# Attention of a fused kernel: both heads of a pair side by side on the array

## The chip, the cores and the metric

The kernel runs on one core of a Trainium2 chip. The metric is the device time of one execution in microseconds, measured on that core, as the median of several runs.

## What is computed

Three stages follow each other. The inputs q, k and v have 2 batches, 8 heads, 576 places and 64 dimensions a head, in float32.

```python
def _attn_ref(q, k, v):
    ...
    q_rot, k_rot = (rotate(q), rotate(k))
    scale = 1.0 / np.sqrt(D)
    scores = scale * np.matmul(q_rot, k_rot.transpose(0, 1, 3, 2))
    scores = scores - np.max(scores, axis=-1, keepdims=True)
    attn = np.exp(scores)
    attn = attn / (np.sum(attn, axis=-1, keepdims=True) + 1e-09)
    return np.matmul(attn, v).astype(np.float32)
...
def _moe_ref(x, w_in, w_out):
    h = x @ w_in
    g = np.maximum(0.01 * h, h)
    return (g @ w_out).astype(np.float32)
```

`rotate` turns the two halves of a head's dimensions by cosine and sine of the place. The attention output, 1152 rows of 512, goes through the dense stage above (512 to 2048 to 512), and then through eight experts (512 to 1024 to 512), of which each row takes the two with the largest noisy logits. The change touches attention alone.

## The kernel before

Attention works on eight pairs of heads (`NP = B * 4`). A pair's q and k are loaded (`load_qk`), turned by place on VectorE or GpSimd (`rope`, letters O and P), transposed on TensorE (`turn`, Q and K), and split into a high part on ScalarE (`turn_high`, h and i) and a rest on VectorE (`turn_low`, j and n), both in float32r, a float32 that TensorE reads in one pass. TensorE contracts over 128 rows, a head has 64 dimensions. So `TQ` and `TK` hold a head's parts twice, in the upper and the lower 64 rows: high and low of q against two copies of high k, then low k against a second copy of high q, with the row of negated maxima below it. The second copies are made by DMA (`turn_copy`, a and b).

The work on a tile of 128 keys or queries, in steps:

- `max_scores` (M), line 386: scores with queries as rows, two matmuls of 288 columns; `max_reduce` (D), line 393, takes the negated maximum on VectorE.
- `max_turn` (R), lines 403 to 408, makes the column of maxima a row; `max_rows` (m) and `max_put` (e) bring it into `TQ`.
- `scores` (S), line 437: keys as rows, two products for each half of 288 queries. `exp` (W), line 443, on ScalarE.
- `values` (V), line 456: float32, 128 keys against 128 columns, of which 64 are values and 64 are ones, so that the sums come out beside the values. A float32 matmul stands in the trace as two passes.
- `take` (U), `sums` (t), `invert` (T), `sums_out` (s), `sums_in` (B), `normalize` (N), `x_high` and `x_low` (X, Y): divide by the sums and write the dense stage's input. Of the last pair, T, s, B and N are queued in the dense stage, at its second step, X and Y at the third.

Maxima, scores and turned tiles take turns in three buffers of PSUM (the digit behind a letter). The order of all engines' work in attention is written out by hand in the string `ORDER`, a letter for each step, and each engine runs its own instructions in that order. The order brings the maxima of the next pair in between the scores and values of this one. Weights of the dense stage are loaded and converted under it (F, and the signs at the end). Pair 0 starts apart: VectorE turns its head 0 and GpSimd its head 1; TensorE runs `busy` matmuls on zeros meanwhile (line 140).

Of the kernel before, what the change touches and what calls it, by code (L numbers as in the profile page):

```python
# [45 lines left out]
def constants():  # L46
# [11 lines left out]
    for j in range(KT):  # L58
        ok = p if j < 4 else p[:64]
        s = 4 * ok + j if j < 4 else 512 + ok  # L60
        ct[ok, j] = np.concatenate([cos[s], cos[s]], 1)
        st[ok, j] = np.concatenate([-sin[s], sin[s]], 1)
# [20 lines left out]
def fused_kernel(ctx, tc, q, k, v, w_in, w_out, w_gate, w_noise, noise, w1, w2, consts, out):  # L83
# [59 lines left out]
    NSLOT = 12  # L143
    slots = [[epool.tile([128, 2, 512], F32R, name=f"w{n}_0") for n in "hl"]]
    KQ, KK = 2 * 2 * KT * 128, 2 * 2 * S
    last_set = [epool.tile([128, n], F32R, name=f"set_{x}") for x, n in (("q", KQ), ("k", KK))]
    for t in last_set:
        slots.append([t[:, o:o + 1024].rearrange("p (a b) -> p a b", a=2) for o in (0, 1024)])
# [83 lines left out]
    NSET = 3  # L232
# [4 lines left out]
    raw, TQ, TK, VF, VT = [], [], [], [], []  # L237
    for i in range(NSET):
        if i < 2:
            TQ.append(ap.tile([128, 2, 2, KT * 128], F32R, name=f"TQ{i}"))  # L240
            TK.append(ap.tile([128, 2, 2, S], F32R, name=f"TK{i}"))
        else:
            TQ.append(last_set[0].rearrange("p (a w n) -> p a w n", a=2, w=2))
            TK.append(last_set[1].rearrange("p (a w n) -> p a w n", a=2, w=2))
    maxes = []
    for i in range(2):
        raw.append({n: ap.tile([128, 2, KT, D], F32, name=f"raw_{n}{i}") for n in "qk"})
        VF.append(ap.tile([128, 4, 192], F32, name=f"VF{i}"))
        VT.append(ap.tile([128, 2, 128], F32, name=f"VT{i}"))
        maxes.append(ap.tile([128, 9], F32R, name=f"maxes{i}"))  # L250

    def fill(eng, t, v):
        if eng == "A":
            src = (one if v else zero)[:t.shape[0]]
            for _ in t.shape[2:]:
                src = src[:, :, None]
            A.copy(t, src.to_broadcast(t.shape))
        else:
            (V if eng == "D" else G).memset(f32(t), v)

    def fill_raw(i, n):
        G.memset(raw[i][n][64:128, :, 4, :], 0.0)

    def fill_t(i, n):
        t, v = ((TQ[i][0:64, 1, 1, :], 0.0), (TK[i][0:64, 1, 1, :], 0.0), (TK[i][64:65, 0, 1, :], 1.0),
                (TK[i][0:1, 1, 1, :], 1.0))[n]
        fill(FILL_T[i], t, v)

    def fill_v(i, n):

        t, v = ((VF[i][:, :, 64:128], 1.0), (VT[i][0:64, 0, 64:128], 1.0), (VT[i][64:128, 0, :], 0.0),
                (VT[i][64:128, 1, 0:64], 1.0), (VT[i][0:64, 1, :], 0.0))[n]
        fill(FILL_V[i], t, v)

    def load_qk(pr, n, part, a=slice(0, 2), queue=None):

        b, h0 = divmod(pr, 4)
        h0 *= 2
        src, t = q if n == "q" else k, raw[pr % 2][n]
        base = src.offset + (b * H + h0 + a.start) * S * D  # L280
        heads = [S * D, a.stop - a.start]
        if part == 0:
            (queue or nc.sync).dma_start(t[:, a, 0:4, :].rearrange("p h j d -> p h (j d)"),
                                         bass.AP(tensor=src.tensor, offset=base, ap=[[4 * D, 128], heads, [1, 4 * D]]))
        else:
            (queue or nc.sync).dma_start(t[0:64, a, 4, :],
                                         bass.AP(tensor=src.tensor, offset=base + 512 * D, ap=[[D, 64], heads, [1, D]]))

    def load_v(pr, part):
# [3 lines left out]
        if part < 2:  # L293
            nc.sync.dma_start(VF[pr % 2][:, :, part * 128:part * 128 + 64],
                              bass.AP(tensor=v.tensor, offset=base + part * S * D, ap=[[4 * D, 128], [D, 4], [1, D]]))
        else:
            a = part - 2
            nc.sync.dma_start(VT[pr % 2][a * 64:a * 64 + 64, a, a * 64:a * 64 + 64],
# [21 lines left out]
    pause = ap.tile([1, 1], F32, name="pause")  # L320

    def after_first():

        G.tensor_copy(pause, roped[0, "k"][0][0:1, 0, 0, 0:1])

# [4 lines left out]

    def turn(pr, n, a, at):


        r = roped[pr, n][0]
        p = ps(at, "pT", (128, 1024))
# [5 lines left out]
        for b in range(2) if a is None else (a,):  # L341
            turned[pr, n, b] = p

    def sides(a):
        return slice(64 * a, 64 * a + 64), slice(64 - 64 * a, 128 - 64 * a)

    def turn_high(pr, n, a):
        here = sides(a)[0]
        A.activation((TQ if n == "q" else TK)[pr % NSET][here, a, 0, 0:S], turned[pr, n, a][here, 0:S], AF.Copy)

    def turn_copy(pr, n, a):
        here, there = sides(a)
        t = (TQ if n == "q" else TK)[pr % NSET]
        if (pr, n) == (0, "k"):
            A.activation(t[there, a, 0, 0:S], turned[pr, n, a][here, 0:S], AF.Copy)
        elif n == "k":
            nc.sync.dma_start(f32(t)[there, a, 0, :], f32(t)[here, a, 0, :])
        else:
            nc.sync.dma_start(f32(t)[here, a, 1, 0:S], f32(t)[here, a, 0, 0:S])

    def turn_low(pr, n, a):
        here, there = sides(a)
        t = (TQ if n == "q" else TK)[pr % NSET]
        o = t[there, a, 0, 0:S] if n == "q" else t[here, a, 1, :]
        V.tensor_tensor(o, turned[pr, n, a][here, 0:S], f32(t)[here, a, 0, 0:S], op=OP.subtract)  # L365

    def tiles(pr):
        last = ((0, 4), (1, 4)) if pr == 0 else ((None, 4),)  # L370
        return [(0, j) for j in range(4)] + list(last) + [(1, j) for j in range(4)]

    def part(a, j):

        if j < 4:
            return ((a, j * 128, 128),), slice(0, 128)
        return (((1, 448, 128), (0, 512, 64)) if a is None else ((0, 512, 64),) if a == 0 else ((1, 448, 128),),
                slice(0, 128) if a is None else slice(64 * a, 64 * a + 64))

    maxed = {}  # L380
# [8 lines left out]
    def max_reduce(pr, a, j):  # L389
        rows = part(a, j)[1]  # L390
        i = 4 if j == 4 else j if a == 0 else 5 + j
        with nc.allow_low_precision(reason="what is taken off is the same in a row's every place"):
            V.tensor_reduce(maxes[pr % 2][rows, i:i + 1], maxed.pop((pr, a, j))[rows, :, 0:288], axis=AX.XY, op=OP.max,  # L393
                            negate=True)
# [3 lines left out]
    def max_turn(pr, a, at):  # L398
        m = maxes[pr % 2]
        if (pr, a) in DIRECT:  # L400
            p = rows[pr, a] = ps(at, "pR", (128, 1024))
            for j in range(4):
                T.matmul(p[:1, j * 128:(j + 1) * 128], m[:, 5 * a + j:5 * a + j + 1], ident_r, start=True, stop=True)
            r = slice(64 * a, 64 * a + 64)
            T.matmul(p[:1, 512:576], m[r, 4:5], ident_r[r, r], start=True, stop=True)
        else:
            p = rows[pr, a] = ps(at, "pR", (128, 128), F32R)
            T.transpose(p[:5, :], m[:, 4 * a:4 * a + 5], ident_r)

    def max_rows(pr, a):  # L410
        o = 64 - 64 * a
        if (pr, a) in DIRECT:
            A.activation(TQ[pr % NSET][o:o + 1, a, 1, 0:S], rows[pr, a][:1, 0:S], AF.Copy)
        else:
            mr = a2.tile([16, 128], F32R, name="mr")
            A.activation(mr[:5], f32(rows[pr, a])[:5], AF.Copy)
            rows[pr, a] = mr

    def max_put(pr, a, w):
        t, mr = f32(TQ[pr % NSET]), f32(rows[pr, a])  # L420
        if a == 0:
            nc.sync.dma_start(t[64:65, 0, 1, :].rearrange("o (j n) -> o j n", j=KT), mr[0:5, :])
        elif w == 0:
            nc.sync.dma_start(t[0:1, 1, 1, 0:512].rearrange("o (j n) -> o j n", j=4), mr[1:5, :])
        else:
            nc.sync.dma_start(t[0:1, 1, 1, 512:576], mr[0:1, 64:128])
# [754 lines left out]
```

## Time and profile before

| | |
|---|---|
| median of 3 runs | 663.74 us (663.44 to 664.36) |
| span of the profiled execution | 663.5 us |
| TensorE busy | 641.5 us, 97% |
| VectorE, ScalarE, GpSimd busy | 394.5, 318.7, 166.3 us |
| attention, first maxima to last values | 9.9 to 175.6 us |

The profiled execution is one run; its span is from the first to the last instruction, and the runs' median lies 0.2 us above it. A busy engine in this table is one that has an instruction in flight. TensorE's matmuls overlap in the listing, so busy time is not the same as streaming time: the distance from one start to the next says what a matmul costs.

### The profile page before, as it was taken

What the parts mean: (1) busy time and instruction counts of PE and PEld (TensorE: products, weight loads), DVE (VectorE), ACT (ScalarE), POOL (GpSimd) and SP (SyncE); (2) the same over time, 40 slices, a digit from 0 to 9 for tenths busy, and PEclk for the clock granted to TensorE, in tenths of its full rate; (3) what the DMA queues carried; (4) which work ended last, traced back from release to release, by engine and by line L of the source; (5) the groups of instructions that cost most, each with busy time, mean ns of one, the idle gap of its engine ahead of it and who ended that gap; (6) DMA issues with size and microseconds to landing.
All of it is one profiled execution on the core that took longest, in us unless ns stands there. A gap on an engine that the chain in (4) does not pass through costs nothing. (4 is left out here: it accounts for less than half of the span.)

```text
span 663.5 us, 10447 instructions
## 1 busy us (share of the span) xinstructions
PE 641.5 (97%) x3676; PEld 552.9 (83%) x3680; DVE 394.5 (59%) x835; ACT 318.7 (48%) x646; POOL 166.3 (25%) x176
## 2 busy tenths in 40 slices
PE   7999999999999999999999999999999999999993
PEld 4778888888878888889799966888888888888893
DVE  8754554687269888853146663565565656475611
ACT  5455554676545554432235432545454545454511
POOL 7985555121130000000000003041505050505102
PEclk9899999999999999999999999999999999999998
DMA  6434422666358443310355432566658584757423
GB/s 172 119 89 120 101 65 67 178 187 196 114 180 301 142 127 126 112 33 1 116 191 154 119 103 61 160 158 185 174 169 201 157 211 146 193 158 197 101 31 42
DMA packets 88903, 90.56 MB, mean 136 GB/s; under 512 B 21455, under 2 KB 66702, under 8 KB 88846
## 3 DMA queue, kind: packets, MB, share of 16 engines
q1 hardware_dynamic: 83502, 78.67, 40.3%
q0 software_dynamic: 4608, 10.49, 8.0%
q10 hardware_dynamic: 736, 0.69, 0.3%
q8 instruction: 30, 0.49, 0.3%
q14 instruction: 27, 0.22, 0.1%
HBM read 69.95 MB, written 14.19 MB: 127 GB/s over the span
## 5 line engine op out<-in xcount | busy, mean ns | idle before, releaser
L218 DVE TENSOR_TENSOR wl<-raw,wh 128x512 fp32r<-128x512 f32 x108 | 72.6, 688 | 53.3 <-ACT wh L216 49.4
L1036 POOL DMA_INDIRECT out<-y_row,idx x24 | 41.9, 1744 | 174.4 <-ACT y_row L1023 169.5
L216 ACT ACTIVATE wh<-raw 128x512 fp32r<-128x512 f32 x108 | 66.4, 629 | 37.1 <-DMA raw<-in_moe_w 36.5
L393 DVE TENSOR_REDUCE maxes<-pM 128x1 fp32r<-128x576 f32 (+1 forms) x73 | 53.9, 754 | 44.5 <-PE pM L386 43.8
L903 POOL DMA_INDIRECT got<-x_rows,idx x24 | 25.1, 1046 | 215.8 <-DVE load L853 199.7
L1012 PE MATMUL bank<-wh,g_x 128*128 128x512 f32 x216 | 78.0, 403 | 0.2
L456 PE MATMUL pO<-p,VF 128*128 128x288 f32 x256 | 72.4, 409 | 0.8 <-ACT p L443 0.8
L443 ACT ACTIVATE p<-pS 128x576 f32<-128x576 f32 (+1 forms) x73 | 46.6, 650 | 51.7 <-PE pS L437 51.0
L599 PE MATMUL bank<-xe_h,wl 128*128 128x320 f32 x216 | 67.0, 311 | 0.0
L599 PE MATMUL bank<-xe_h,wh 128*128 128x320 f32 x216 | 66.8, 310 | 0.0
L599 PE MATMUL bank<-xe_l,wh 128*128 128x320 f32 x216 | 66.3, 309 | 0.0
L620 ACT ACTIVATE g_t<-bank 128x512 f32<-128x512 f32 (+2 forms) x48 | 23.5, 490 | 86.3 <-PE bank L599 86.3
L621 DVE TENSOR_TENSOR g_f<-bank,g_t 128x512 f32<-128x512 f32 (+2 forms) x48 | 26.7, 557 | 50.1 <-ACT g_t L620 49.8
L456 PEld LDWEIGHTS pO<-p,VF 128*128 128x128 f32 x256 | 45.4, 190 | 9.7 <-ACT p L443 1.3
L599 PE MATMUL bank<-xh,wh 128*128 128x384 f32 (+2 forms) x152 | 51.6, 340 | 1.4 <-ACT xh L506 1.4
L608 PE MATMUL bank<-g_h,wh 128*128 128x384 f32 (+2 forms) x152 | 51.9, 341 | 0.0
L599 PE MATMUL bank<-xl,wh 128*128 128x384 f32 (+2 forms) x152 | 51.3, 338 | 0.2 <-POOL xl L512 0.2
L599 PE MATMUL bank<-xh,wl 128*128 128x384 f32 (+2 forms) x152 | 51.4, 338 | 0.0
L608 PE MATMUL bank<-g_l,wh 128*128 128x384 f32 (+2 forms) x152 | 51.3, 337 | 0.0
L608 PE MATMUL bank<-g_h,wl 128*128 128x384 f32 (+2 forms) x152 | 51.0, 336 | 0.0
L1012 PEld LDWEIGHTS bank<-wh,g_x 128*128 128x128 f32 x216 | 40.5, 188 | 7.9 <-DVE g_x L995 0.5
L437 PE MATMUL pS<-TQ,TK 128*128 128x288 f32 (+1 forms) x240 | 45.2, 319 | 1.8 <-DVE TQ L365 0.9
(240 smaller groups left out, 1470.1 us busy)
## 6 DMA issues: line engine op xcount, KB each, us to landing
raw<-in_moe_w SPq DMA_DIRECT2D x128, 256.0 KB
raw<-in_moe_w_in SPq DMA_DIRECT2D x16, 512.0 KB
raw<-in_moe_w_out SPq DMA_DIRECT2D x16, 512.0 KB
inv_sum<-inv_sums SPq DMA_DIRECT2D x16, 144.0 KB
out<-none SPq DMA_DIRECT2D x9, 256.0 KB
VF<-in_v SPq DMA_DIRECT2D x16, 128.0 KB
wl<-kept SPq DMA_DIRECT2D x4, 512.0 KB
wh<-kept SPq DMA_DIRECT2D x4, 512.0 KB
```

Of the source, the lines that this page charges most:

```text
L216: A.activation(hi[:, part], t, AF.Copy)
L218: V.tensor_tensor(lo[:, part], t, f32(hi)[:, part], op=OP.subtract)
L393: V.tensor_reduce(maxes[pr % 2][rows, i:i + 1], maxed.pop((pr, a, j))[rows, :, 0:288], axis=AX.XY, op=OP.max, negate=True)
L437: T.matmul(p[:m, z, 0:288], tk[:r, b, w, c:c + m], tq[:r, b, w, z * 288:(z + 1) * 288], start=(w == 0), stop=(w == 1), skip_group_check=True)
L443: A.activation(t[r], scored.pop((pr, a, j))[r, :, 0:288], AF.Exp, scale=0.125)
L456: T.matmul(acc[g][:, z, 0:288], w, p[r, z, :], start=opens, stop=closes)
L599: T.matmul(h[:, :n], w[:, 0, k * 128:(k + 1) * 128], m[:, k, cols:cols + n], start=(i == 0), stop=(i == 11))
L608: T.matmul(b[:, o:o + n], w[:, 1, ds], m[:, :n], start=(first and opens and t == 0), stop=(last and t == 2), skip_group_check=True)
L621: V.tensor_tensor(g[:, :n], h[:, :n], t[:, :n], op=OP.max)
L903: G.indirect_dma_start(out=t[:n], out_offset=None, in_=x1_rows, in_offset=bass.IndirectOffsetOnAxis(ap=idx[e][:n, st:st + 1], axis=0))
L1012: T.matmul(yr[st], s, w, start=(f == 0 and t == 0), stop=(f == 7 and t == 2))
L1036: s = G.indirect_dma_start(out=out, out_offset=bass.IndirectOffsetOnAxis(ap=idx[e][:n, st:st + 1], axis=0), in_=r[:n], in_offset=None, com ...
```

## The change

Two heads of a pair lie beside each other, head 0 in rows 0 to 63 and head 1 in rows 64 to 127 of one `high` and one `low` tile for each of q and k. No part is stored twice.

- Maxima and scores are matmuls on 64 rows. Each comes twice in a row, once for each head, on the two halves of the rows and into two banks of PSUM. Maxima now come from the high parts alone, and of pairs 1 to 7 in column pieces of 320 and 256. Scores are four products: high with high, low q, low k, and a matrix of ones with the row of maxima `MR`.
- Values are four float32 matmuls of 32 columns each, two for each head, in four places of the array's columns. Ones no longer stand beside the values: sums are matmuls of their own against `add_up`, 144 columns wide, again four side by side.
- One `take`, one copy of sums and no `turn_copy` or `max_put` are left of those steps. Constant tiles are filled on GpSimd. GpSimd turns all pairs from pair 1 on, VectorE also head 1's q of pair 0. The last pair's T, s and B are queued one dense step sooner. `ORDER` is new.

```diff
-    def max_scores(pr, a, j, at):
-        p = maxed[pr, a, j] = ps(at, "pM")
-        for b, c, m in part(a, j)[0]:
-            for z in range(2):
-                T.matmul(p[:m, z, 0:288], TQ[pr % NSET][:, b, 0, c:c + m],
-                         TK[pr % NSET][:, b, 0, z * 288:(z + 1) * 288], start=True, stop=True, skip_group_check=True)
+    def here(a):
+        return slice(0, 128) if a is None else slice(64 * a, 64 * a + 64)
...
+    def max_scores(pr, i, j, at):
+        p = maxed[pr, i, j] = ps(at, "pM")
+        hq, hk = high["q"][pr % NSET], high["k"][pr % NSET].rearrange("p (j w n) -> p j w n", j=KT, w=2)
+        for a, z in ((i, 0), (i, 1)) if pr == 0 else ((0, i), (1, i)):
+            o = (192, 0)[z] if pr == 0 else 0
+            n = (320, 256)[z]
+            T.matmul(p[:, z if pr == 0 else a, o:o + n], hq[here(a), j * 128:(j + 1) * 128],
+                     hk[here(a), 0:KT - z, (a + z) % 2], start=True, stop=True)
...
+    def max_turn(pr, at):
+        p = rows[pr] = ps(at, "pR", (128, 1024))
+        for j in range(KT):
+            T.matmul(p[:65, j * 128:(j + 1) * 128], peak[pr % 2][:, j], ident_r, start=True, stop=True)
...
-    def scores(pr, a, j, at):
-        tq, tk = TQ[pr % NSET], TK[pr % NSET]
-        p = scored[pr, a, j] = ps(at, "pS")
-        for b, c, m in part(a, j)[0]:
-            for w in range(2):
-                r = 65 if w == 1 and b == 0 else 128
-                for z in range(2):
-                    T.matmul(p[:m, z, 0:288], tk[:r, b, w, c:c + m], tq[:r, b, w, z * 288:(z + 1) * 288],
-                             start=(w == 0), stop=(w == 1), skip_group_check=True)
+    def products(pr, j):
+        i = pr % NSET
+        cs = slice(j * 128, j * 128 + 128)
+        return ((high["k"][i][:, cs], high["q"][i]), (high["k"][i][:, cs], low["q"][i]),
+                (low["k"][i][:, cs], high["q"][i]), (ones[:, int(j == 4)], MR[pr % 2]))
+    def scores(pr, j, z, at):
+        p = scored[pr, j, z] = ps(at, "pS")
+        cols = slice(z * 288, z * 288 + 288)
+        ws = products(pr, j)
+        for t, (w, x) in enumerate(ws):
+            for a in range(2):
+                T.matmul(p[:, a, 0:288], w[here(a)], x[here(a), cols], start=(t == 0), stop=(t == 3))
...
-        w = VF[pr % 2][:, j, 64 * a:64 * a + 128] if j < 4 else VT[pr % 2][r, a, :]
-        for z in range(2):
-            T.matmul(acc[g][:, z, 0:288], w, p[r, z, :], start=opens, stop=closes)
+        for a in range(2):
+            for c in range(2):
+                w = VF[pr % 2][:, a, j] if j < 4 else VT[pr % 2][:, a]
+                r = slice(64 * a + 32 * c, 64 * a + 32 * c + 32)
+                T.matmul(y[r, z, 0:288], w[:, 32 * c:32 * c + 32], prob[pr, j, z][:, a], start=(j == 0), stop=False, skip_group_check=True)
+        for o in range(2 * z):
+            for a in range(2):
+                for c in range(2):
+                    r = slice(64 * a + 32 * c, 64 * a + 32 * c + 32)
+                    T.matmul(y[r, o, 288:432], add_up[:, 0 if j < 4 else 1 + a], prob[pr, j, c][:, a, o * 144:o * 144 + 144],
+                             start=False, stop=(j == 4), skip_group_check=True)
...
-    DIRECT, ROPE_V = ((0, 0), (0, 1)), ((1, 'q'),)
     ORDER = (
-"cucluyuluyulxffyflfxzykzxkzIxkzkvlOvvOlvOlvOOoooooooooooooooooQ0lOwOhOwjpPooK1aPwiOwbnPwooooM2M0PwDM1wPDQ2wPDM"
+"kkfoooooooockckIkfkkkffOOOOPOlQ0OOolPOhOlPK1PlooilM2M0PDK1oOOiOPDlQ2PnZM0hwPDM1FDM0FPDM1ZDlM0ZjPM1!lDQ2PlDM0hw"
...
-            "I": (lambda: V.tensor_copy(ident_r, ident), [()]),
+            "I": (lambda: A.copy(ident_r, ident), [()]),
...
     base = 82
-    for n in "Ts":
-        sched(base + 1, work[n][0], NP - 1)
-    for n in range(2):
-        sched(base + 1, sums_in, NP - 1, n)
+    for n in "TsB":
+        sched(base, work[n][0], NP - 1)
     sched(base + 1, normalize, NP - 1)
```

**In the midst of attention, on TensorE.** Before, while pair 0's scores and values (`TQ_113`, `TK_114`) run among pair 1's maxima (`TQ_115`, `TK_116`), each row a program step (a values row of two stands for two float32 matmuls):

```order
L386 MATMUL pM<-TK_116,TQ_115 128x288 x4
L437 MATMUL pS<-TQ_113,TK_114 128x288 x4
L456 MATMUL pO<-p,VF_119 128x288 x2
L386 MATMUL pM<-TK_116,TQ_115 128x288 x4
L437 MATMUL pS<-TQ_113,TK_114 64x288 x4
L456 MATMUL pO<-p,VF_119 128x288 x2
```

After, pair 0's scores and values among pair 2's maxima (`high_k_120`):

```order
L345 MATMUL pM<-high_k_120,high_q_117 128x320 x2
L388 MATMUL pS<-high_q_115,high_k_118 128x288 x2
L388 MATMUL pS<-low_q_121,high_k_118 128x288 x2
L388 MATMUL pS<-high_q_115,low_k_124 128x288 x2
L388 MATMUL pS<-MR_134,ones 128x288 x2
L345 MATMUL pM<-high_k_120,high_q_117 128x256 x2
L405 MATMUL pO<-p,VF_131 32x288 x4
L345 MATMUL pM<-high_k_120,high_q_117 128x320 x2
...
L405 MATMUL pO<-p,VF_131 32x288 x4
L410 MATMUL pO<-p,add_up 32x144 x8
```

Four score matmuls became eight, in twos, and two values matmuls became four of 32 columns, with eight sums behind every second group; work on 64 rows and work on 32 columns take turns.

**Where the first scores stand, on TensorE.** Before, behind pair 0's maxima:

```order
L403 MATMUL pR<-ident_r,maxes_121 1x128 x4
L405 MATMUL pR<-ident_r,maxes_121 1x64
L386 MATMUL pM<-TK_114,TQ_113 128x288 x10
L437 MATMUL pS<-TQ_113,TK_114 128x288 x4
L340 MATMUL pT<-ct,rope_k 128x128 x5
```

After (`rope_k` is pair 1's, `high_k_119` made from it):

```order
L322 MATMUL pT<-ct,rope_k 128x128 x5
L368 MATMUL pR<-ident_r,peak_133 65x128 x5
L139 LDWEIGHTS warm
L139 MATMUL pW<-warm 128x512
L345 MATMUL pM<-high_k_119,high_q_116 128x320 x2
L388 MATMUL pS<-high_q_115,high_k_118 128x288 x2
```

The transposes of pair 1's k moved from behind the first scores to ahead of them, with pair 1's first maxima.

**ScalarE's queue at the start.** Before, head 1's loads stand among fills:

```order
L536 DMA ct<-in_constants 128x128
L257 CAST TQ_113<-zero 64x640
L257 CAST TK_114<-zero 64x576
L283 DMA raw_q_117<-in_q 128x256
```

After:

```order
L483 DMA ct<-in_constants 128x128
L489 CAST ident_r<-ct 128x128
L268 DMA raw_q_129<-in_q 128x256
L272 DMA raw_q_129<-in_q 64x64
L268 DMA raw_k_130<-in_k 128x256
```

The copy of the identity, which reads the constants, moved from VectorE to ScalarE, ahead of head 1's loads.

## Rows read from the trace of the kernel before

**Rows 1.** The page's busy time of engines over the span.

```profile
PE 641.5 (97%) x3676; PEld 552.9 (83%) x3680; DVE 394.5 (59%) x835; ACT 318.7 (48%) x646; POOL 166.3 (25%) x176
```

**Rows 2.** Busy time by stage: length, engines, granted clock, DMA share, GB/s.

```profile
9.90:19.35 9.45, 6.93 (x36) 4.56 (x37) 9.29 (x14) 2.58 (x4) 9.29 (x10) 0.96 0.46 118
19.35:175.60 156.25, 153.11 (x871) 131.67 (x871) 90.04 (x132) 89.44 (x151) 75.62 (x63) 0.99 0.47 129
175.60:230.00 54.40, 52.83 (x281) 44.88 (x280) 43.84 (x85) 28.42 (x55) 6.92 (x11) 1.00 0.58 186
```

**Rows 3.** Waits of TensorE in attention, first and last of nine: us, times, longest.

```profile
PE pS L437 <- DVE TQ L365: 1.4, 3, 0.5
...
PE pT L340 <- DVE maxes L393: 0.2, 1, 0.2
```

**Rows 4.** Timeline of TensorE's matmuls from 90 us: start, us, line, form, count.

```profile
90.08 0.69 PE L386 MATMUL pM<-TK,TQ 128*128 128x288 f32 x4
90.61 1.13 PE L456 MATMUL pO<-p,VF 128*128 128x288 f32 x4
91.37 0.64 PE L386 MATMUL pM<-TK,TQ 128*128 128x288 f32 x2
91.85 0.22 PE L408 MATMUL pR<-ident_r,maxes 128*5 128x128 f32 x1
91.91 0.34 PE L437 MATMUL pS<-TQ,TK 128*128 128x288 f32 x1
```

**Rows 5.** Groups by form: busy us, mean ns of one.

```profile
L456 PE MATMUL pO<-p,VF 128*128 128x288 f32 x256 | 72.4, 409 | 0.8 <-ACT p L443 0.8
```

**Rows 6.** Timeline of TensorE's matmuls around a step on 64 rows.

```profile
32.28 0.42 PE L386 MATMUL pM<-TK,TQ 128*128 128x288 f32 x2
32.63 1.23 PE L456 MATMUL pO<-p,VT 64*128 64x288 f32 x4
...
34.18 0.30 PE L437 MATMUL pS<-TQ,TK 128*128 128x288 f32 x1
```

**Rows 7.** Timeline of TensorE's weight loads in the same stretch.

```profile
32.02 0.19 PEld L437 LDWEIGHTS pS<-TQ,TK 128*128 128x128 f32 x1
...
33.80 0.30 PEld L386 LDWEIGHTS pM<-TK,TQ 128*128 128x128 f32 x2
```

**Rows 8.** Timeline of TensorE around the router's logits, float32 under 16 columns.

```profile
315.50 0.34 PE L599 MATMUL bank<-xh,wl 128*128 128x384 f32 x1
315.67 0.34 PE L599 MATMUL bank<-xl,wh 128*128 128x384 f32 x1
315.94 1.46 PE L733 MATMUL bank<-x,wgn 128*16 128x512 f32 x3
...
320.03 1.24 PE L733 MATMUL bank<-x,wgn 128*16 128x256 f32 x5
321.20 0.44 PE L608 MATMUL bank<-g_h,wh 128*128 128x384 f32 x1
321.48 0.34 PE L608 MATMUL bank<-g_h,wl 128*128 128x384 f32 x1
```

**Rows 9.** Timeline of the first 20 us, all engines.

```profile
1.24 0.45 ACTq L536 DMA_DIRECT2D ct<-in_constants  x1
4.25 0.69 DVE L541 CAST ident_r<-ct 128x128 fp32r<-128x128 f32 x1 [0.29 <-DMA ct<-in_constants]
10.94 0.86 POOL L313 TENSOR_TENSOR rope_k<-raw_k,ct_att 128x320 f32<-128x320 f32 x1
13.68 1.54 POOL L313 TENSOR_TENSOR rope_k<-raw_k,ct_att 128x640 f32<-128x640 f32 x1
17.18 1.55 POOL L318 TENSOR_TENSOR rope_k<-rope_k,rope_t 128x640 f32<-128x640 f32 x1
19.35 1.33 PE L437 MATMUL pS<-TQ,TK 128*128 128x288 f32 x4
```

**Rows 10.** Groups on TensorE from 176 to 200 us.

```profile
L599 PE MATMUL bank<-xh,wh 128*128 128x512 f32 (+1 forms) x11 | 4.0, 363 | 1.4 <-ACT xh L506 1.4
```

**Rows 11.** Timeline of VectorE in the dense stage.

```profile
182.96 0.20 DVE L479 RECIPROCAL rc<-rc 128x9 f32<-128x9 f32 x1
```

More of the change, by code (lines that the diff above doesn't have):

```diff
@@ L236, in fused_kernel @@
     att.enter_context(tc.manual_schedule(engines={ET.SP}))
[L237 to L245, printed above, removed]
+    W = {"q": S, "k": KT * 128}
@@ L249, in fused_kernel @@
[L249 to L262, printed above, removed]
@@ L361, in turn_low @@
[L361 to L378, printed above, removed]
@@ new lines, in fused_kernel, with max_join, max_rows @@
+    rows = {}
+    def max_join(pr):
+        with nc.allow_low_precision(reason="what is taken off is the same in a row's every place"):
+            V.tensor_tensor(peak[pr % 2][:, :, 0:65:64].rearrange("p j h -> p h j"), halves[pr, 0], halves[pr, 1], op=OP.min)
+    def max_turn(pr, at):
+        p = rows[pr] = ps(at, "pR", (128, 1024))
+        for j in range(KT):
+            T.matmul(p[:65, j * 128:(j + 1) * 128], peak[pr % 2][:, j], ident_r, start=True, stop=True)
+    def max_rows(pr):
+        A.activation(MR[pr % 2][:65], rows[pr][:65, 0:S], AF.Copy)
@@ L552, in fused_kernel @@
-            "R": (max_turn, heads), "m": (max_rows, heads),
-            "e": (max_put, [(pr, a, w) for pr, a in heads if (pr, a) not in DIRECT for w in range(a + 1)]),
-            "V": (values, [(pr, a, j) for pr in range(NP) for a, js in enumerate((range(5), (4, 0, 1, 2, 3))) for j in js]),
-            "U": (take, [(g,) for g in range(2 * NP)]),
-            "t": (sums, [(pr, n) for pr in range(NP) for n in range(3)]),
-            "B": (sums_in, [(pr, n) for pr in range(NP) for n in range(2)]),
@@ new lines, in fused_kernel @@
+            "I": (lambda: A.copy(ident_r, ident), [()]),
+            "O": (rope, [(0, n, V, i, a, a + 1) for n, a in FIRST_V for i in range(4)] +
+                  [(pr, n, V, i) for pr, n in pairs[2:] if (pr, n) in ROPE_V for i in range(4)]),
+            "P": (rope, [(0, n, G, i, a, a + 1) for n, a in FIRST_G for i in range(4)] +
+                  [(pr, n, G, i) for pr, n in pairs[2:] if (pr, n) not in ROPE_V for i in range(4)]),
+            "Q": (turn, [(0, "q", 0), (0, "q", 1)] + [(pr, "q", None) for pr in some]),
@@ new lines, in fused_kernel @@
+            "K": (turn, [(0, "k", 0), (0, "k", 1)] + [(pr, "k", None) for pr in some]),
+            "w": (load_v, [(pr, i) for pr in range(NP) for i in range(3)]),
+            "M": (max_scores, [(0, a, j) for a in range(2) for j in range(KT)] +
+                  [(pr, z, j) for pr in some for j in range(KT) for z in range(2)]),
+            "S": (scores, cells), "W": (exp, cells), "V": (values, cells),
+            "Z": (load_small, [(i,) for i in range(7)]), "F": (load_part, [(p,) for p in range(2 * NEARLY)])}
@@ L560, in fused_kernel @@
+    work["D"] = (max_reduce, work["M"][1])
+    for n, m, x in (("h", "j", "q"), ("i", "n", "k")):
+        work[n] = (turn_high, [(0, x, 0), (0, x, 1)] + [(pr, x, None) for pr in some])
+        work[m] = (turn_low, [(pr, x) for pr in range(NP)])
+    for n, f in (("R", max_turn), ("m", max_rows), ("U", take), ("t", sums), ("T", invert), ("s", sums_out), ("B", sums_in),
+                 ("N", normalize), ("X", x_high), ("Y", x_low)):
         work[n] = (f, [(pr,) for pr in range(NP)])
-    for i, n in enumerate("xyz"):
-        work[n] = (fill_t, [(i, m) for m in range(4)])
```

239 lines of the change are left out of this document (95 added, 144 removed).

## The prediction

> **What bounds the kernel now.** I read the whole first, then the stages, then the waits, then single instructions. Over the span TensorE is busy 97% [rows 1], so the question is what TensorE does, not what the others do. By stage [rows 2], attention runs from the first maxima at 9.9 to the last values at 175.6, in 9.45 + 156.25 = 165.7 us. From the first scores (19.35) on, TensorE is busy 153.11 of 156.25, while VectorE has 90.0, ScalarE 89.4 and GpSimd 75.6 us of work. The waits of TensorE in the whole stage are nine groups and sum to 6.0 us, from 1.4 for the longest to 0.2 for the least [rows 3]. So a microsecond of TensorE's own time saved in attention should come off the span, and a slower VectorE or ScalarE has over 60 us of room before it binds. The dense stage behind it is as full of TensorE, reads its weights in the same order as now, and should only be shifted. The granted clock is 0.96 in the head and 0.99 or 1.00 of 2.4 GHz after it [rows 2], so I price everything at the full clock.
>
> **What one instruction costs.** Matmuls overlap in the listing, so the price is the distance from start to start. Four score or max matmuls of 288 columns take 0.69 us together [rows 4] and one alone 0.30 [rows 6]: (0.69 - 0.30) / 3 = 0.13, and I use 0.132. A float32 values matmul is two passes; four passes take 1.13 [rows 4], one 0.409 [rows 5]: (1.13 - 0.41) / 3 = 0.24; I use 0.242. With 64 rows a pass costs the same, four take 1.23 including the way in [rows 6]: half an array is not faster, it only leaves the other half empty.
>
> **The change, term by term.**
>
> *Maxima.* Before: 8 pairs x 20 matmuls of 288 columns; the first pair's lie in the head, 140 x 0.132 = 18.5 us remain. After: for pairs 1 to 7, 70 couples, one matmul on rows 0 to 63 and its twin on 64 to 127, 35 of 320 columns (0.145 by the same slope) and 35 of 256 (0.119). If twins run side by side, 9.2 us: -9.3.
>
> *Scores.* Before 8 x 40 = 320 matmuls, 42.2 us. After 640 on half the rows each, 320 couples at 0.133: 42.6, +0.4. The third and fourth products take the place that the second copy of a head took in the rows.
>
> *Values and sums.* Before 160 matmuls, 320 passes x 0.242 = 77.4 us; half their columns hold ones. After: 80 groups of four matmuls, one for each 32 columns of the array, 288 wide, and 80 groups of four sums, 144 wide. If four stand side by side, a group costs two passes: 80 x 0.484 + 80 x 0.242 = 58.1, so -19.3.
>
> *The cut of the array.* Before, nearly all work uses the whole array. After, maxima and scores use it in halves of rows and values in quarters of columns, and the order goes to and fro: counted in the built order, 49 entries into the quarters, 48 into the halves, 16 back to the whole. The trace has prices. Two maxima start at 32.28; the second, 0.13 later, should be followed at 32.54 by the 64-row values, but these start at 32.63, and their four passes take 1.23 instead of 1.13 [rows 4, 6]: 0.09 + 0.10 = 0.19. The router's 16-column float32 matmuls start 0.27 after the last whole one where 0.17 is usual [rows 8]: 0.10. The way back: five passes of 256 columns from 320.03, at 0.242 x 256 / 288 = 0.215 each, should end at 321.11; the next whole matmul starts at 321.20, the second 0.28 behind it instead of 0.17 [rows 8]: 0.09 + 0.11 = 0.20. The lower end is nothing: the 5-column max rows at 91.85 stand 0.13 behind the maxima and 0.06 before the scores [rows 4]. I take the dear rows, because they have the forms of the new work (64 rows; float32 under 32 columns): 49 x 0.10 + 48 x 0.19 + 16 x 0.20 = 17.2, less two 64-row visits of before, in and out at 0.3 each: +16.6.
>
> *Turning the maxima.* 22 small matmuls before, 40 of 128 columns after, at the 0.06 of [rows 4]: +1.1.
>
> *What costs nothing.* The copies of heads by DMA, the max rows by DMA, two of three sum copies, half the turned copies on ScalarE go; seven more exponentials, seven joins of half-maxima and the rope of pair 1's q (to GpSimd) come. All of it stands under TensorE's 153 us [rows 2]; it would cost itself only if attention fell under some 100 us.
>
> *The head.* Pair 0's first scores are queued in TensorE's order behind the first maxima of pair 1, and those behind pair 1's k. GpSimd now ropes head 1's k, then pair 1's q, then its k. ScalarE's copy of the identity now stands before head 1's four loads on its queue; that copy can start when the constants land, at 4.25, 3.0 us after their issue at 1.24 [rows 9]. Four issues of some 0.4 and a landing as long as that give 8.5. The half-size rope takes 13.68 - 10.94 = 2.74, a whole one 17.18 + 1.55 - 13.68 = 5.05 [rows 9]: 8.5 + 2.74 + 2 x 5.05 = 21.4. Turning and copying add 1.4, the maxima 0.3: first scores at 23.1 instead of 19.35 [rows 9]. Of these 3.75, 0.8 is TensorE work done earlier than now: +3.0. (Bounds: 0, if the loads are sooner; 5.)
>
> *The tail.* TensorE waits 1.4 us for the last pair's output in the dense stage [rows 10]. The reciprocal on that chain runs at 182.96 [rows 11], 7 us after the last values, since it is queued behind the second dense step's work on VectorE; the change queues it a step sooner: -1.4.
>
> Sum: -9.3 + 0.4 - 19.3 + 16.6 + 1.1 + 3.0 - 1.4 = -8.9. The span is 663.5 and the median of the runs 663.74, so what lies around the span is 0.2; 663.7 - 8.9 = **654.8 us.** By its own range of the cut (0.1 to 0.2 an entry) and head: 646 to 661.
>
> **The rivals.** All turn on what the trace of before has nowhere, two matmuls at once; its rows bound that from one side, that half an array is no faster by itself. That tiles overlap in full is my choice, with the chance below.
>
> *Faster: the changes of cut cost nothing,* as with the 5-column rows. Then 16.6 less: 638. Against it: both float32 visits pay.
>
> *No change:* the head at its 5 and waits for exponentials between small groups eat the gain: 662 to 665.
>
> *Slower: weights one after the other.* Two weight loads of 128 columns start (0.30 - 0.19) = 0.11 apart when nothing hides them [rows 7]; I use 0.108. A couple of scores needs two in the 0.133 it streams. If loads for the two halves queue up, a couple costs 0.216: 320 x 0.083 + 35 x 0.071 + 35 x 0.097 = 32.4, giving 687. It decides as soon as a couple costs more than 0.133 + 8.9 / 320 = 0.161. For it: loads of one part do queue so. Against: the halves are loaded from different partitions.
>
> *Slower: passes in order.* Each float32 matmul is two passes on the same quarter, and the next quarter stands behind both. If starts keep the program's order, the second pass waits 0.242 for the first and holds back the next matmul; only neighbours overlap, four matmuls cost four passes, not two: +58.1, 713. In this trace starts follow the program's order everywhere. The Trainium skill (TensorE: Matmul & The Clock Gate, "What overlaps and what doesn't") says that matmuls start and end in strict order, with tiles overlapping all the same; by that rule this rival's 713 would be the sum, and no run so far shows a pass held back between tiles.
>
> *Slower: overlap in part.* If the quarters reach four fifths of their overlap, values cost 58.1 / 0.8 = 72.6, +14.5: 669. The same page's "Measured speedup vs the span model" gives 2.38 for three column tiles, 0.79 of full; by it the sum would be about 670.
>
> *Nothing overlaps:* couples +42 and +9, values +174: 880. The trace does not exclude it.
>
> **How the numbers follow.** The forecast 0.54, cuts free 0.10, no change 0.05, weights in a row 0.13, overlap in part 0.07, passes in order 0.08, nothing overlaps 0.03. Predicted is the likeliest, 654.8. Faster by over 0.2% (1.3 us, about what a measurement of this kernel can tell): 0.64; within it 0.05; slower 0.31. The range reaches from free cuts to weights in a row, 637 to 688, and leaves out the last two and edges; the forecast's own is 646 to 661.
>
> **What would show it.** Attention's end should move from 175.6 to about 167. Right: score matmuls start in couples, 0.133 a couple; four values matmuls start together, a group of four near 0.5 us; 0.1 to 0.2 us gaps at each change between them; first scores near 23; no wait for the last pair's output. Wrong: couples 0.2 apart with weight loads end to end (weights in a row), values passes 0.24 apart (in order), no gaps (cuts free). It is also wrong if TensorE idles for more than 10 us in attention, since then another engine sets the pace.

## The result, and the profile after

Four runs of the changed kernel have a median of 658.12 us (655.18 to 659.61), against 664.05 (663.44 to 666.04) for four of before: ratio 0.9889, 95% interval 0.9856 to 0.9922. The same kernel run once more gave 656.21 and 0.9863 (0.9838 to 0.9888). The medians are 5.9 and 8.3 us apart (before has 664.46 beside the second); the ratios, which are not the quotients of the medians, say 7.4 and 9.1. So the change is worth some 6 to 9 us of the forecast 8.9, and 658.12 lies inside the forecast's own range of 646 to 661. The profiled span went from 663.5 to 655.7.

By stage (start and end, length, busy time and count of PE, PEld, DVE, ACT and POOL, granted clock, DMA share, GB/s), cut at the first maxima, the first scores and the last values:

```profile
0.00:9.80 9.80, 7.13 (x21) 2.96 (x22) 3.73 (x14) 2.94 (x5) 5.18 (x33) 1.00 0.57 160
9.80:26.28 16.48, 13.24 (x53) 9.31 (x52) 13.56 (x18) 3.91 (x6) 15.74 (x16) 0.61 0.60 172
26.28:168.61 142.33, 138.84 (x2156) 98.81 (x2154) 93.30 (x126) 76.09 (x125) 75.15 (x60) 1.00 0.30 95
168.61:655.70 487.09, 473.57 (x2740) 413.02 (x2740) 289.85 (x671) 219.59 (x477) 73.93 (x82) 0.99 0.50 138
```

Beside [rows 2]: the first scores come 6.9 us later (26.28, not 19.35). From them to the last values it takes 142.3 instead of 156.3, 13.9 less. The rest changes by 0.8. TensorE is busy 138.8 of the 142.3 us between first scores and last values, so its own time still sets that stretch. The second row, the head, changed for the worse: it takes 16.5 us instead of 9.45, GpSimd is busy nearly all of it as before (15.7 us), and the granted clock is 0.61 instead of 0.96. (It is at the lower of its two levels, 1.2 GHz, from 13.5 to 27.2, after TensorE had waited 1.7 us for a rope, the turning of a k by place.)

TensorE in attention, in order of time:

```profile
29.39 0.29 PE L388 MATMUL pS<-high_q,high_k 64*128 64x288 f32 x2
29.52 0.29 PE L388 MATMUL pS<-low_q,high_k 64*128 64x288 f32 x2
29.65 0.29 PE L388 MATMUL pS<-high_q,low_k 64*128 64x288 f32 x2
29.78 0.29 PE L388 MATMUL pS<-MR,ones 64*128 64x288 f32 x2
29.91 0.31 PE L345 MATMUL pM<-high_k,high_q 64*128 64x320 f32 x2
30.15 0.69 PE L405 MATMUL pO<-p,VF 128*32 128x288 f32 x8
30.66 0.67 PE L410 MATMUL pO<-p,add_up 128*32 128x144 f32 x16
31.27 0.38 PE L345 MATMUL pM<-high_k,high_q 64*128 64x256 f32 x2
31.49 0.29 PE L388 MATMUL pS<-high_q,high_k 64*128 64x288 f32 x2
```

Read the starts. Scores come in couples (x2) 0.13 apart, as priced. The eight passes of a values group, four matmuls of two, take 30.66 - 30.15 = 0.51, not 1.94: all four quarters run at once. The group's sums, 16 passes in four lots, are followed 0.61 later. Within a lot the four starts in the trace are 7 ns apart.

The weight loads of the same couples:

```profile
29.39 0.19 PEld L388 LDWEIGHTS pS<-low_q,high_k 64*128 64x128 f32 x2
29.52 0.19 PEld L388 LDWEIGHTS pS<-high_q,low_k 64*128 64x128 f32 x2
```

Two loads take 0.19 together where two whole ones took 0.30 [rows 7]: the halves load side by side.

Waits of TensorE from 9.8 to 180 us, the longest ones (in all, times, longest):

```profile
PE pS L388 <- DVE half L357: 2.8, 2, 2.5
PE pT L322 <- POOL rope_k L304: 1.7, 1, 1.7
PE pT L322 <- DVE rope_q L304: 1.0, 1, 1.0
PE bank L550 <- DVE g_l L570: 0.8, 1, 0.8
```

The wait for the last pair's output, xh [rows 10], is gone; a wait of 0.8 for g_l, in the dense stage too, is new.

The rows that end the head (timeline):

```profile
9.63 0.86 POOL L299 TENSOR_TENSOR rope_k<-raw_k,ct_att 128x320 f32<-128x320 f32 x1 [3.44 <-DMA raw_k<-in_k]
...
20.32 1.41 DVE L352 TENSOR_REDUCE peak<-pM 128x1 fp32r<-128x576 f32 x2
20.57 1.33 PE L322 MATMUL pT<-ct,rope_q 128*128 128x128 f32 x5
20.89 1.54 POOL L304 TENSOR_TENSOR rope_k<-rope_k,rope_t 128x640 f32<-128x640 f32 x1
21.83 1.33 PE L345 MATMUL pM<-high_k,high_q 64*128 64x320 f32 x4
...
22.71 1.42 DVE L352 TENSOR_REDUCE peak<-pM 128x1 fp32r<-128x576 f32 x2 [0.98 <-PE pM L345]
...
23.62 1.30 PE L322 MATMUL pT<-ct,rope_k 128*128 128x128 f32 x5
...
24.57 0.89 PE L368 MATMUL pR<-ident_r,peak 128*65 128x128 f32 x5
...
25.56 0.65 ACT L371 ACTIVATE MR<-pR 65x576 fp32r<-65x576 f32 x1
```

Three things end here almost together: pair 1's k (22.43), pair 0's ten reductions (24.1; they stand in a row on VectorE, and a couple of scores needs the maxima of both heads), and TensorE at half clock.

### The profile page after: what moved, and what is told of

The parts are those of the page before. It is cut to its first block, busy times and chain, and to the rows that moved or that the text cites. A ratio compares the mean times of both kernels' runs of the same rounds, so it can differ in the third digit from the quotient of the medians.

```text
span 655.7 us, 12763 instructions
## 1 busy us (share of the span) xinstructions
PE 632.8 (97%) x4964; PEld 524.1 (80%) x4965; DVE 400.4 (61%) x828; ACT 302.5 (46%) x613; POOL 170.0 (26%) x189
## 5 line engine op out<-in xcount | busy, mean ns | idle before, releaser
L213 DVE TENSOR_TENSOR wl<-raw,wh 128x512 fp32r<-128x512 f32 x128 | 86.1, 689 | 62.7 <-ACT wh L211 53.4
L392 ACT ACTIVATE p<-pS 128x576 f32<-128x576 f32 x80 | 49.3, 650 | 46.4 <-PE pS L388 46.4
L550 PE MATMUL bank<-g_l,wh 128*128 128x512 f32 (+2 forms) x192 | 64.7, 337 | 0.8 <-DVE g_l L570 0.8
L550 PE MATMUL bank<-g_h,wh 128*128 128x512 f32 (+2 forms) x192 | 65.4, 340 | 0.0
L541 PE MATMUL bank<-xh,wh 128*128 128x512 f32 (+2 forms) x192 | 65.0, 338 | 0.0
L541 PE MATMUL bank<-xh,wl 128*128 128x512 f32 (+2 forms) x192 | 64.9, 338 | 0.0
L357 DVE TENSOR_REDUCE half<-pM 128x2 f32<-128x640 f32 x70 | 51.3, 755 | 21.9 <-PE pM L345 21.3
L541 PE MATMUL bank<-xl,wh 128*128 128x512 f32 (+2 forms) x192 | 64.7, 337 | 0.0
L550 PE MATMUL bank<-g_h,wl 128*128 128x512 f32 (+2 forms) x192 | 64.5, 336 | 0.0
L541 PEld LDWEIGHTS bank<-xe_h,wh 128*128 128x128 f32 x256 | 48.3, 188 | 5.9 <-ACT xe_h L856 0.2
L954 PE MATMUL bank<-wl,g_x 128*128 128x512 f32 x128 | 50.0, 391 | 0.0
```

What stands on the lines that cost most here:

```text
L213: V.tensor_tensor(lo[:, part], t, f32(hi)[:, part], op=OP.subtract)
L357: V.tensor_reduce(halves[pr, i][:, :, j], p[:, :, :(320, 256)[i]], axis=AX.X, op=OP.max, negate=True)
L392: A.activation(t, scored.pop((pr, j, z))[:, :, 0:288], AF.Exp, scale=0.125)
L541: T.matmul(h[:, :n], w[:, 0, k * 128:(k + 1) * 128], m[:, k, cols:cols + n], start=(i == 0), stop=(i == 11))
L550: T.matmul(b[:, o:o + n], w[:, 1, ds], m[:, :n], start=(first and opens and t == 0), stop=(last and t == 2), skip_group_check=True)
L954: T.matmul(yr[st], s, w, start=(f == 0 and t == 0), stop=(f == 7 and t == 2))
```

## The experiments

All ran against before. Ratios of the changed kernel itself are 0.9889 and 0.9863. The letters of the order: M a maximum, D its reduction, Q and K turn q and k, R the row of maxima, m its copy, S scores, W exponentials, V values, k loads, I the copy of the identity, o a busy matmul (on zeros, for the clock alone).

**What sets the head.** Four runs. First, head 1's loads ahead of the identity:

```diff
-"kkfoooooooockckIkfkkkff
+"kkfoooooooockckkfkkkIff
```

> Theory A (the head is set by the late loads of head 1): the copy of the identity no longer stands ahead of the loads, head 1's k lands some 2 us sooner than at 9.6, GpSimd's three ropes end some 2 us sooner, first scores near 24.3 instead of 26.3, time 1.5 to 2.5 us under the changed kernel. Theory B (the head is set by TensorE at half clock and by the reduces on VectorE, one after the other): GpSimd ends sooner, the first scores move by under 0.7 us, the time by under 0.7 us.

Measured: 656.49 us, 0.9873 (0.9855 to 0.9892), first scores at 26.40. The ropes did end sooner, pair 1's k at 20.47 instead of 22.43, but its turn on TensorE started at 23.62 as in the changed kernel. So the late loads alone do not set the head.

Second, 41 busy matmuls more, wherever TensorE waits in the head (a part):

```diff
-K1PlooilM2M0PDK1oOOiOPDlQ2PnZM0hwPDM1FDM0F
+K1PlooooilM2M0oooooPDK1ooooOOiOPDlQ2ooPnZM0ohwPDM1ooFDM0ooF
...
-Q2PlDM0hwPDM1lolDPK0
+Q2ooPlDM0oohwPDM1loooooolDPK0
```

> 41 matmuls on zeros more while TensorE waits in the head. Theory B: the granted clock stays at 2.4 GHz between 13 and 27 us, transposes of pair 1's k start when its rope ends (22.4), first scores near 24.7, time 1.5 to 2 us under the changed kernel. Theory A: the clock stays up, the first scores stay within 0.7 us of 26.3 and the time stays, or is longer by the matmuls that stand in the way.

Measured: 654.61, 0.9852 (0.9834 to 0.987). Its windows row over the head:

```profile
9.80:26.30 16.50, 15.29 (x80) 7.75 (x78) 13.87 (x18) 3.67 (x6) 16.18 (x16) 1.00 0.58 158
```

The clock is whole, and yet the first scores stand at 26.58. What the run gained lies elsewhere (first scores to last values 141.3, 1.0 less, and 2.4 less behind them), in stretches that vary by about as much between two profiles of the changed kernel. Third, both together:

> Both edits. If loads and clock each hold a part, the gains add: first scores near 22.5, time 3 to 4 us under the changed kernel. If one of them alone sets the head, no more than that one gives alone.

Measured: 653.52, 0.9825 (0.9807 to 0.9844), first scores at 26.33. With loads and clock out of the way, the ten reductions, TensorE's order and the busy matmuls themselves are left. Their chain in this run:

```profile
19.08 1.55 POOL L304 TENSOR_TENSOR rope_k<-rope_k,rope_t 128x640 f32<-128x640 f32 x1
...
22.09 0.76 DVE L352 TENSOR_REDUCE peak<-pM 128x1 fp32r<-128x576 f32 x1 [1.22 <-PE pM L345]
...
22.99 1.47 PE L139 MATMUL pW<-warm 128*128 128x512 bf16 x6
23.09 0.76 DVE L352 TENSOR_REDUCE peak<-pM 128x1 fp32r<-128x576 f32 x1 [0.24 <-PE pM L345]
...
24.29 0.71 PE L322 MATMUL pT<-ct,rope_k 128*128 128x128 f32 x5
```

Pair 1's k is roped at 20.63, but its turn stands behind the last maxima and six busy matmuls, and starts at 24.29, although the buffer it writes, the 0 of K0, was read out when the first of these reductions ended, at 22.85. The two reductions themselves waited for TensorE (1.22 and 0.24 us). So in this run and the one before, the busy matmuls that keep the clock up stand in the way of the head, and neither shows what the clock alone is worth there.

Next I put pair 0's row of maxima ahead of pair 1's turns, and pair 1's first maxima behind the first scores:

```diff
-M0ZjPM1!lDQ2PlDM0hwPDM1lolDPK0w#R1jliolPmnM2lPS1DlS0W
+M1ZPM2!lDM0PlDM2wPDlolDPR1moQ0K2hwijlS1#lPnS0lPWM2lW
```

> The changed kernel with another order of the head alone: pair 1's turns of q and k and its first maxima stand behind pair 0's row of maxima and its first scores, and the ten maxima of pair 0 use three banks in turn. Theory B (a couple of scores needs the maxima of both heads, and these ten stand in a row on TensorE at half clock and on VectorE): the last reduction of pair 0 ends 1.2 to 2 us sooner than at 24.1, the first scores stand at 24.4 to 25.5 instead of 26.28, and the whole is 1 to 2 us shorter than the changed kernel, ratio about 0.986. Rival (TensorE is short of nothing but work and clock there: what is put off comes back behind the first scores): first scores earlier by up to 2 us, last values unmoved within 0.5 us, ratio 0.989 as it was.

Measured: 657.97, 0.9894 (0.9877 to 0.9911); first scores at 25.75, 0.5 sooner, last values at 170.31. This profile has a stretch of 3.4 us at half clock at 114.7 as well. The edit does less than its expectation says: Q0 and K2, the turns of pair 1's q and k, still stand ahead of S1.

```profile
23.48 1.27 PE L322 MATMUL pT<-ct,rope_q 128*128 128x128 f32 x5
24.54 1.27 PE L322 MATMUL pT<-ct,rope_k 128*128 128x128 f32 x5
25.75 0.48 PE L388 MATMUL pS<-high_q,high_k 64*128 64x288 f32 x2
```

The copy of the row of maxima ended at 23.98, and the scores waited behind these turns until 25.75. The ratio is the rival's (the last values came 1.7 later than in the changed kernel), but the order that was meant was not tried. Last, all three together (23 busy matmuls more, fewer than before, since I left most out between the maxima; here S stands ahead of pair 1's K, though still behind its Q):

> All that the head showed, together: head 1's loads ahead of the identity, 23 more busy matmuls where TensorE waits, pair 0's row of maxima and scores ahead of pair 1's turns and maxima, and three banks for pair 0's maxima. Theory H (the late first scores have three covers, one under the other: loads, half clock, and the row of ten reductions that both heads' maxima need; only all three together move them): no half clock in the head, first scores near 23.5 instead of 26.3, 2 to 3 us less than with loads and busy matmuls alone, ratio 0.978 to 0.980. Rival (what is put off comes back behind the first scores, as in the run with the order alone): ratio 0.982 to 0.984.

Measured: 657.32, 0.9878 (0.9853 to 0.9904). The clock fell all the same, from 18.8 to 29.0, so this run does not tell Theory H from its rival. First scores came at 25.43, and from them to the last values took 148.5 us, in a profile that is the slowest of its six runs (662.03). What sets the head stays open: the late loads alone do not, and for the clock and the order no run here decides. The head also varies by itself: in the second profile of the changed kernel the first scores stand at 25.93, and in the next run, whose head is the same and whose clock was whole from 15.5 to 18.9, at 25.16.

**Whose order do starts keep?** Scores of a cell written as four products of head 0, then four of head 1:

```diff
-        for t, (w, x) in enumerate(ws):
-            for a in range(2):
+        for a in range(2):
+            for t, (w, x) in enumerate(ws):
```

> Four products of head 0, then four of head 1, in place of head by head in turn; same work. Theory C (matmuls start in the program's order): a cell takes seven steps of 0.13 instead of four, +0.39 us in 80 cells, 31 us more. Theory D (each half of the rows has its own order, and a later matmul may start first): a cell still takes four steps, time within 2 us of the changed kernel.

Measured: 659.87, 0.9925 (0.9896 to 0.9954), 1.8 and 3.7 us above the two medians of the changed kernel; first scores to last values 146.20, 3.9 more.

```profile
72.01 0.40 PE L388 MATMUL pS<-low_q,high_k 64*128 64x288 f32 x2
72.14 0.40 PE L388 MATMUL pS<-high_q,low_k 64*128 64x288 f32 x2
72.28 0.40 PE L388 MATMUL pS<-MR,ones 64*128 64x288 f32 x2
```

Two of each product still stand together, every 0.13; the twins are now 0.11 apart (0.40 for two, not 0.29). In the program a product's twin is four matmuls behind it. Started strictly in that order, a cell would take at least six steps of 0.13 (only the fourth product of a head could run beside the first of the other), and it takes four. So Theory C's 31 us are refuted, and here each half of the rows kept an order of its own: a matmul on one passed those that stand ahead of it for the other.

**Are quarters needed?** Values as one product of 64 columns a head, sums left at 32:

```diff
-            for c in range(2):
-                T.matmul(y[r, z, 0:288], w[:, 32 * c:32 * c + 32], prob[pr, j, z][:, a], ...
+            T.matmul(y[64 * a:64 * a + 64, z, 0:288], w, prob[pr, j, z][:, a], ...
```

> The changed kernel with each head's values as one product 64 columns wide, in place of two of 32; the sums stay 32 columns wide. Theory S (parts of the array run side by side at any width that the change uses, and a cell's values take the two passes of 288 columns either way, 0.44 us): the 40 values without sums cost the same; the 40 with sums get a change of width between values and sums and lose 0.1 to 0.35 us each, so 4 to 14 us slower than the changed kernel, ratio 0.995 to 1.010. Rival (float32 with halves of 64 columns runs one after the other): 80 cells by 0.48 us more, 38 us slower, ratio about 1.05.

Measured: 663.61, 0.9993 (0.9976 to 1.0011); first scores to last values 149.50, 7.2 more, inside Theory S.

```profile
85.12 0.71 PE L403 MATMUL pO<-p,VF 128*64 128x288 f32 x4
85.75 0.70 PE L408 MATMUL pO<-p,add_up 128*32 128x144 f32 x16
```

Values to sums is 0.63, where quarters took 0.51. The halves do run side by side (one after the other would, by the price of a pass, be 0.97 and 38 us), but the gain of the change is lost. Adding up the distances from start to start in the two traces, the way from values to sums takes 4.5 us more, from sums to values 1.5, and the values and sums themselves 1.1 and 1.0, while TensorE idles 1.0 less. So most of the 7.2 goes to the new changes of width: 0.343 from a second pass to the sums instead of 0.242, 0.216 back instead of 0.103. Sums on 64 columns as well, with no change of width, were not tried.

**What does a change of cut cost?** Fewer: two, then five values next to each other.

```diff
-S0WPwM2WDM1VDPM0lS2DwM1WVDFPlM0S2PDM1WVPDM0S2DM1WPD
+S0WPwM2WDM1DPM0lS2DwM1WVVDFPlM0S2PDM1WPDM0S2DM1WPD
```

> The changed kernel with the values of a group of keys' two halves of the queries (the second with its sums) next to each other: 33 places at which TensorE goes from 64-row halves to 32-column quarters and back instead of 49. Theory C (a change and the change back cost 0.37 us together, as the trace of the changed kernel reads near 70.5 and 71.5 us): 16 pairs of changes fewer, 5.9 us shorter, first scores to last values 136 to 137 us instead of 142.3, ratio about 0.980. Rival (the changes lie in part beside waits, or the bunched values leave ScalarE and VectorE short of work and then late): less than 2 us, ratio 0.986 to 0.992, and waits of TensorE for VectorE's reductions or ScalarE's exponentials longer by what the changes give.

> As the run by two, with five values next to each other (two groups of a pair): 15 places instead of 49. Theory C: 34 pairs of changes fewer at 0.37 us, 12.6 us shorter, first scores to last values about 130 us, ratio about 0.970. Rival (five values in a row, 2.2 us and more, leave ScalarE and VectorE without new scores and maxima, and the scores behind them wait): no better than by two, or slower; ratio 0.98 to 0.995, with TensorE's idle time between first scores and last values over 6 us instead of 3.5.

Measured: by two 659.28, 0.9914 (0.9898 to 0.993), by five 673.91, 1.018 (1.0139 to 1.0221). First scores to last values 144.77 and 159.15: the rival in both, by five even slower than its 0.98 to 0.995. TensorE's idle time in that stretch is 5.8 and 16.9 us (3.5 in the changed kernel), and these are waits, the first rows by five:

```profile
PE pM L345 <- ACT p L392: 2.9, 7, 0.7
PE pS L388 <- ACT p L392: 2.5, 9, 0.7
```

TensorE waits for exponentials and reductions behind the bunched values, as the rival had it. The price is not confirmed by these runs: without the idle time the stretch takes 139.0 and 142.3, against 138.8 in the changed kernel, although there are 16 and 34 visits fewer. The distances behind values and sums did shrink, from 65.0 to 62.7 and 60.4 us, which is 0.14 a visit, but those behind maxima and scores grew by as much by two and by more by five, idle time left out. So, the other way round, more changes with the same matmuls: the sums behind the next score or maximum.

```diff
-V (values, then sums)  M              S
+V (values)             M  v (sums)    S
```

> The changed kernel with the sums of a group of keys taken out of their place behind the values and put behind the next score or maximum, where another score or maximum follows: 78 visits of TensorE to the 32-column quarters instead of 49, with the same matmuls and no wait added that the trace of the changed kernel would suggest. Theory C (a visit costs 0.10 on the way in and 0.22 on the way out, since the first couple of scores behind it takes 0.235 where 0.13 is usual and stands 0.11 late itself): 29 more by 0.33, 9.6 us longer than the changed kernel, first scores to last values about 152. Rival 1 (only the late starts cost, 0.10 and 0.11; the doubled first couple is made up behind it): 6.1 us longer. Rival 2 (changes are covered, and the time that bunching by two and five lost was lost to the changes being free): within 2 us.

Measured: 667.20, 1.0034 (1.0017 to 1.0051): 9 to 11 us longer than the changed kernel, 0.31 to 0.38 for each of the 29 visits. First scores to last values is 12.0 longer, 1.8 of it in idle time. Theory C: more visits cost what was forecast, though fewer did not give it back.

```profile
30.45 0.38 PE L345 MATMUL pM<-high_k,high_q 64*128 64x256 f32 x2
30.76 0.70 PE L412 MATMUL pO<-p,add_up 128*32 128x144 f32 x16
31.39 0.40 PE L388 MATMUL pS<-high_q,high_k 64*128 64x288 f32 x2
31.62 0.29 PE L388 MATMUL pS<-low_q,high_k 64*128 64x288 f32 x2
31.75 0.30 PE L388 MATMUL pS<-high_q,low_k 64*128 64x288 f32 x2
```

The couple of maxima ahead (0.12 of columns) takes 0.31, the first couple of scores behind takes 0.23 and the second 0.13.

**The longest wait, and a better kernel.** Loads first and warm, and on VectorE a weight conversion behind two reductions near 110 us:

```diff
-* S2 Y ! M0 * V W # V N D W M1 S2 D P S0 W T
+* S2 Y ! M0 V W V N D W M1 S2 D * # P S0 W T
```

> Loads first and 41 busy matmuls in the head, as before, and one more edit: on VectorE the second subtraction and the first clamp of a weight conversion, 1.8 us and the start of the next word, stand behind two reductions of maxima near 110 us instead of ahead of them. Theory W (TensorE's longest wait in attention, 2.5 us at 113.8 in the changed kernel's profile and 1.2 in the run with loads first and busy matmuls, is that conversion and nothing else): the wait is gone, 1 to 2.5 us shorter than that run, ratio 0.979 to 0.981, and no stretch at half clock near 112 to 118, which the profiles of five runs show after it. Rival (the reduction that then stands behind the conversion is late instead): the wait moves by some 5 us and the time stays, ratio 0.982 to 0.984.

Measured: 652.76, 0.9813 (0.9785 to 0.9841), the fastest here, 3.5 to 5.4 us under the changed kernel's two medians. Its waits:

```profile
PE pT L322 <- DVE rope_q L304: 1.2, 1, 1.2
...
PE pS L388 <- DVE half L357: 0.3, 1, 0.3
```

The 1.2 us wait for half (1.5 in two waits, in the run without this edit) is down to 0.3, and first scores to last values is 139.3, 2.1 less than in the run without this edit: Theory W by the profile. The medians are only 0.8 apart, less than its 1 to 2.5, and the ratios of the two runs overlap, so the times do not show it. Nor does the clock: the run without this edit had no half clock there either.

The changed kernel, for a second profile:

> The changed kernel once more, for a second profile beside the others of this chip: if the part behind the last values (487.07 in its first profile, 484.6 to 486.1 in runs that change only the head) varies by itself, it comes out below 486.5; if the head's clock sets it, 487.0 or more. Ratio 0.986 to 0.992.

Measured: 656.21; the part behind the last values took 484.75 instead of 487.07, with the same instructions. It varies by itself by some 2 us, so differences of that size there prove nothing in any of these runs. This profile also has half clock in attention, right behind a 2.1 us wait of TensorE:

```profile
114.10:117.50 3.40, 3.40 (x36) 1.88 (x38) 2.21 (x4) 2.21 (x4) 0.00 (x0) 0.50 0.06 21
```

## Why the prediction was right

**Side by side: right.** Couples at 0.13, four quarters in 0.51, loads of halves together. This refutes weights one after the other, passes in order, overlap in part, and nothing overlaps. The strict order of starts that the Trainium skill states (TensorE: Matmul & The Clock Gate, "What overlaps and what doesn't") does not hold between tiles here. The run with heads in a row took 3.9 us more, where strict order gives at least two steps of 0.133 in each of 80 cells, 21. A values group took 0.51, where it gives four passes, 0.97, if the two passes of a matmul stand next to each other in the program, as the forecast had it and the trace does not tell. The Trainium skill's 2.38 for three column tiles (the same page, "Measured speedup vs the span model") is 0.79 of full; four tiles of another form gave 1.94 / 0.51 = 3.8 here, 0.95 of full.

**Maxima, scores, values and sums, and the cut: -11.6 forecast.** Adding up the distances from each start to the next in the two traces gives, for scores, maxima and values with sums, 51.1 + 25.5 + 68.1 = 144.7 before and 49.0 + 17.0 + 65.0 = 131.0 after: -13.7. The prices give 42.2 + 18.5 + 77.4 = 138.1 and 42.6 + 9.3 + 58.1 + 16.6 = 126.6. So the old kernel lost 6.6 beside its price and the new one 4.4; 1.4 of the former is half clock, granted from 18.7 to 22.1, behind its first scores at 19.35. The rest of this difference I can't place.

**The cut alone: dearer than +16.6.** From the maxima at 29.91 (320 columns, 0.145) to the values at 30.15 there is 0.10 too much, and values to sums 0.51 has 0.03 over two passes: 0.12 in, where I took 0.10. From the sums at 30.66 to the maxima at 31.27 is 0.61, 0.12 over four passes of 0.121; these take 0.22 where 256 columns take 0.12: 0.22 out, where I took 0.19. With the 16 whole ones at the 0.20 that I took: 49 x 0.12 + 48 x 0.22 + 3.2 - 0.6 = 19.0. The step held in kind, 2.4 us short in size; the run with sums apart measures a visit at 0.31 to 0.38, by the rows here 0.34. Cuts free is refuted by that run; bunching the visits did not give the price back.

**The head: the step that failed.** I gave +3.75 to the first scores and they came +6.9 later. The rope's durations held (head 1's k begins at 9.63, not 8.5, and pair 1's k ends at 22.43, not 21.4: 1.0 more; the terms named, 4.25 + 4 x 0.4 + 3.0, give 8.85, not 8.5). The 1.7 from there to the scores was 3.85. The turn of pair 1's k, which I had start at once, stood behind the tenth maxima and a busy matmul until 23.62, and then the turn, the row of maxima and the first scores went at half clock, where I had priced "everything at the full clock". My cause, the loads behind the identity, is refuted as the only one: without them the head stays. How much of the rest is order and how much clock stays open. Of the 6.9, some 1.2 by my estimate is TensorE's work that was done earlier (ten more turns, one couple of maxima), where I took 0.8. So the head cost 5.7 where the sum has 3.0 and its upper bound was 5.

**Turning the maxima, the tail: small and nearly right.** Turns and rows of maxima went from 11.2 to 11.0 where +1.1 for the rows was forecast, ten turns having moved into the head. The reciprocal now runs at 172.93, and the stretch behind the last values is 0.8 shorter, not 1.4, a difference that this stretch also shows by itself. The wait of 0.8 for g_l was not there before: VectorE now runs the reciprocal, 1.03 us instead of the 0.20 of [rows 11], between g_f and g_l of that dense step. That this is the cause is argued, no run shows it.

**The base.** I set 0.2 us around the span, from one execution's span and the median of others. In every profiled run here the time is 1.7 to 1.9 above the span (657.53 for 655.7). So the profiled execution of before was probably one of some 665.3, and the sum from it is 656.4. The saving of 8.9 compares with 7.8 between the two profiled spans. That these are so close is luck in part: the stretch from first scores to last values gave 2.1 more than its prices, and the head took 2.7 more.

## What to carry over

Where heads use half the rows or a quarter of the columns, put them side by side: here matmuls and their weight loads overlapped nearly in full, and the order in which the parts were written was worth 2 to 4 us. Then count the visits to each cut and price them (29 more cost 0.31 to 0.38 us each, there and back), but do not count on getting that back by bunching: by two gave nothing, and five at a time made this kernel some 16 us longer, since the engines that feed TensorE came late. And when a step needs both of two things that came one after the other, look at the head, and read from TensorE's order what a trial really puts ahead of it: busy matmuls for the clock, or turns left in front, can hide what the trial was to show.

## What was not expected of the hardware

A matmul on one half of the rows passed three that stood ahead of it for the other half (twins 0.11 apart, 0.13 per product and half). Behind a change of cut, the second float32 pass of 288 columns started 0.293 behind the first on two 64-column halves and 0.267 on four 32-column quarters; without a change, 0.242 on either. The first couple of fp32r matmuls behind float32 quarters took 0.22 to 0.24, the second 0.13. And the granted clock fell to 0.50 for 3.4 us in the middle of attention, from between 112.5 and 117.8, in five of the thirteen profiles of the changed kernel and its variants, behind waits of 1.5 to 2.1 us (and in the run by five from 132.2); the changed kernel's first profile has a wait of 2.5 at that place and no such fall.
